# First expert's third block of rows with the rows as the stationary side, a first fill of eight steps, and an order table that reaches into the second expert

## The chip, the cores and the metric

One core of a Trainium2 chip runs the whole program. Its engines are TensorE (PE, with its weight loads as PEld), VectorE (DVE), ScalarE (ACT), GpSimd (POOL) and SyncE (SP, which here only starts loads). Each works through its own list in order and waits on semaphores for the others. The metric is the device time of one execution in microseconds (us), as the median of several runs.

## What is computed

Three stages, each on the output of the one before: attention over a window of 64 positions, a dense layer pair, and a mixture of eight experts, of which each token takes one.

```python
# attention: 4 batches x 8 heads x 576 positions x 64; mask 0 <= i - j < 64
attn = softmax(where(mask, q @ k.T / 8, -1e9)) @ v
x = attn.transpose(0, 2, 1, 3).reshape(2304, 512)
# dense pair: 512 -> 2048 -> 512
h = x @ w_in
x = (h * sigmoid(1.702 * h)) @ w_out
# experts: 8 x (512 -> 1024 -> 512)
logits = x @ w_gate
e = argmax(logits); gate = max of softmax(logits)
out[token] = gate * (max(x @ w1[e], 0) @ w2[e])
```

## The kernel before

All large products are made in three matmuls: each operand is split into a high part and a low part of the 32-bit type that TensorE takes, and hi x hi, hi x lo and lo x hi are added up in PSUM (`mm3`, and `mm3_rows` for several blocks of rows that share a weight). ScalarE makes the high part by a copy, VectorE the low part by a subtraction.

Tokens go through attention and the dense pair in nine chunks of 256. A chunk's sixteen steps are `up_mm` (12 matmuls of 256 columns), the activation (`tanh`, `act`, `g_hi`, `g_lo`) and, two steps later, `down` (6 matmuls of 512 columns). Each chunk's rows are then routed and scattered by POOL to a buffer in HBM, `xbuf`, ordered by expert. The experts are taken in the order of their size, which VectorE works out (`pick_first` after seven chunks, `pick_order` after the last). Their room is `CAPS` = 384, 352, 352, 288, 288, 256, 256, 256 rows.

For an expert, SyncE loads its rows (`load_rows`, into `xg`) and its weights in eight pieces of 512 KB (`load_expert`, into the staging tile `ws`; pieces 0, 1, 4, 5 are of `w1`, the others of `w2`). TensorE transposes the rows (`rows_t`), ScalarE and VectorE split them into `eh` and `el` and the weights into `whi` and `wlo`. Eight steps m follow, one for each 128 of the 1024 hidden units: `e_up` (12 matmuls, weights stationary, as many columns as there are rows), `e_act` and `e_rest` (`gh`, `gl`), and two steps later `e_down` (3 matmuls of 512 columns for each block of 128 rows). `e_out` scales a block by its gate and POOL writes it to the output with an indirect DMA.

The order of the work on PE, ACT, DVE and POOL up to the hand-over is written out by a planner: `part(slot, function, arguments, after=...)` registers each piece of work, and `plan` lays them out one by one by the costs in `MODEL` (engine, us, PSUM banks taken and given back). Behind the planned list a plain loop takes the steps of the experts in order.

The first 256 rows of the first expert belong to chunks that are done early, so `SPLIT` = 7 of its steps are in the planned list with 256 columns, where they fill the time in which the last chunk is routed. Its third block of 128 rows is complete only after the last chunk's scatter (`last_rows`). The loop then takes step 7 with all 384 columns, and for the third block the seven earlier steps once more, over 256 columns of which the first 128 are dropped, with 3 matmuls of `e_down` each:

```python
        steps = [(0, m, 0, CAPS[0], 0) for m in range(SPLIT, NF)]
        steps += [(0, m, CAPS[0] - 256, CAPS[0], 256 - (CAPS[0] - CH)) for m in range(SPLIT)]
        steps += [(e, m, 0, CAPS[e], 0) for e in range(1, E) for m in range(NF)]
```

The second expert's rows and its first two pieces of weights are requested once the planned list is through, behind the readings of the expert order for the experts that are left (`which`); its weights are split inside the loop, one piece a step (`prep_both`).

Of the kernel before, what the change touches and what calls it, by code (L numbers as in the profile page):

```python
# [28 lines left out]
E = 8  # L29
# [11 lines left out]
SPLIT = 7  # L41
# [9 lines left out]
def tile_model(  # L51
# [106 lines left out]
    def mm3_rows(rows, a, b):  # L158

        for o, s, first, _ in rows:  # L160
            nc.tensor.matmul(out=o, lhsT=a[0][:, s], rhs=b[0], start=first, stop=False)  # L161
            nc.tensor.matmul(out=o, lhsT=a[0][:, s], rhs=b[1], start=False, stop=False)  # L162
        for o, s, _, last in rows:
            nc.tensor.matmul(out=o, lhsT=a[1][:, s], rhs=b[0], start=False, stop=last)  # L164
# [230 lines left out]
    def down(c, m):  # L395
        if m == 0:
            y_t[c] = [ps.tile([P, DM], F32, tag="ps", name="y") for _ in range(2)]
        gh, gl = g_t.pop((c, m))
        hi, lo = wout_t[m // 4]
        mm3_rows(  # L400
            [(y_t[c][b], slice(b * P, b * P + P), m == 0, m == NM - 1) for b in range(2)],
            (gh, gl), (hi[:, m % 4, :], lo[:, m % 4, :]),
        )
# [220 lines left out]
    def load_expert(e, i):  # L624

        j, z = divmod(i, 2)
# [12 lines left out]
    def prep_expert(e, i, h, lo_eng):  # L639
        j, z = divmod(i, 2)  # L640
        hi, lo = ew_t[e, j]
        split(hi[:, 2 * z + h], lo[:, 2 * z + h], st_t[e, i][:, h], lo_eng)
# [63 lines left out]
    def e_up(e, m, c0=0, c1=None, skip=0):  # L706
# [14 lines left out]
        eu_t[e, m] = (h, n, skip, c0, c1)  # L721

    def e_act(e, m):
        h, n, skip, c0, c1 = eu_t[e, m]
        if "o" in xp2:
            pool, w, n_b = xp2["o"], CAPS[0], 3
        else:
            pool, w, n_b = gp, CH, 3
        if tail(e):
            n -= TAIL  # L730
            if m == 0:
                gt_t[e] = xp2["o"].tile([P, NF, TAIL], F32, tag="gt", name="gt", bufs=1)
# [52 lines left out]
    def e_down(e, m):  # L785
        done, rows = [], []
        gh, gl, c0, c1 = g_t.pop(("e", e, m))
        hi, lo = ew_t[e, 2 * (m // 4) + 1]
        for b, n in blocks(e):
            if not c0 <= b * P < c1:  # L790
                continue
# [6 lines left out]
            rows.append((o[0:n], slice(b * P - c0, b * P - c0 + n), i == 0, i == NF - 1))  # L798
        mm3_rows(rows, (gh, gl), (hi[:, m % 4, :], lo[:, m % 4, :]))
# [208 lines left out]

    def clear_rows():
        with tc.issue_after(last_w[0].ins):  # L1010
            init_xbuf(yp.tile([P, ROW], F32, tag="ys", name="zt"))
# [7 lines left out]
        top_half: ("ACT", 0.66, 0, 0), join: ("DVE", 0.69, 0, 0), w_hi: ("ACT", 0.66, 0, 0), w_lo: ("DVE", 0.67, 0, 0),  # L1019
        up_mm: ("PE", 1.45, 1, 0), tanh: ("ACT", 0.35, 0, 0), act: ("DVE", 0.37, 0, 1),  # L1020
        g_hi: ("ACT", 0.4, 0, 0), g_lo: ("DVE", 0.4, 0, 0), down: ("PE", 1.4, 0, 0),
# [4 lines left out]
        logits_pe: ("PE", 1.0, 0, 0), lg_out: ("DVE", 0.2, 0, 1),  # L1026
# [4 lines left out]
        e_up: ("PE", 1.45, 1, 0), e_act: ("ACT", 0.4, 0, 0), e_rest: ("DVE", 0.4, 0, 1),  # L1031
        e_down: ("PE", 1.4, 0, 0),
        load_gate: ("SP", 6.0, 0, 0), clear_rows: ("POOL", 1.0, 0, 0), swap_pools: ("NONE", 0, 0, 0),
    }
# [6 lines left out]
    def plan():  # L1041
# [5 lines left out]
        while left:  # L1047
# [3 lines left out]
            for k in left:  # L1051
                eng, cost, take, give = MODEL[k[0]]
                take += 2 * (k[0] in (down, e_down) and k[1][1] == 0)
                if k[0] is logits_pe:
# [144 lines left out]
    for m in range(SPLIT):  # L1199
# [18 lines left out]
    for b, _ in blocks(0)[2:]:  # L1218
        part(SLOTS + SPLIT + 0.5, rows_t, 0, b, after=[(last_rows, ())])
        part(SLOTS + SPLIT + 0.6, rows_hi, 0, b, after=[(rows_t, (0, b))])  # L1220
        part(SLOTS + SPLIT + 0.7, rows_lo, 0, b, after=[(rows_hi, (0, b))])

    with tc.manual_schedule(engines={mybir.EngineType.PE}):
# [9 lines left out]
        p2_cm = pools[0]  # L1233
        xpool_cm.__exit__(None, None, None)
        yt_cm.__exit__(None, None, None)
        gp_cm.__exit__(None, None, None)
        p2o_cm = tc.tile_pool(name="p2o", bufs=1, side="right", reuse_waits="tile")
        xp2["o"] = p2o_cm.__enter__()
        count_rows(*cnt_t["order"])
        with tc.issue_after(rows_in[-1].ins):  # L1240
            load_rows(1)
            for i in range(2):
                load_expert(1, i)
        steps = [(0, m, 0, CAPS[0], 0) for m in range(SPLIT, NF)]
        steps += [(0, m, CAPS[0] - 256, CAPS[0], 256 - (CAPS[0] - CH)) for m in range(SPLIT)]
        steps += [(e, m, 0, CAPS[e], 0) for e in range(1, E) for m in range(NF)]
        for i in range(E * NF + 2):
            if i == 2:
                staged.__exit__(None, None, None)
            e = i // NF  # L1250
            if e < E:
                e_up(*steps[i])
                e_act(*steps[i][0:2])
                e_rest(*steps[i][0:2])
            if i > 1:
                e_down(*steps[i - 2][0:2])
            f = (i - 2) // NF
            if i > 1 and tail(f) and (i - 2) % NF == NF - 1:
# [14 lines left out]
        p2_cm.__exit__(None, None, None)  # L1273
        p2o_cm.__exit__(None, None, None)
# [56 lines left out]
```

## Time and profile before

| | |
|---|---|
| median of 3 runs | 735.07 us (734.48 to 737.21) |
| profiled execution, its own time | 736.32 us |
| its span, first to last instruction | 734.5 us |
| TensorE busy | 711.6 us, 97% |
| VectorE, ScalarE, POOL busy | 470.7, 358.2, 47.0 us |
| granted TensorE clock, mean | 0.998 |

The profiled execution is one of its own; its time is the span and what lies around it. The page has the busy time of each engine, the chain that ended last, and the costliest groups of instructions; other views list the waits, a stretch in order of time, or the loads. A matmul's own length (0.28 us for 256 columns, 0.40 for 512) is not its price: they overlap, and what one adds is the distance to the next one's start.

### The profile page before, as it was taken

The page shows a single profiled execution, that of the slowest core. Times are in us where ns is not written, and L with a number is a line of the kernel's source. Part 1 is how long each engine was busy: PE and PEld are TensorE (multiplying, and loading weights), DVE is VectorE, ACT ScalarE, POOL GpSimd, SP SyncE. Part 2 cuts the span into 40 slices and gives each one's busy share as a digit, 9 for nine tenths or more (in the row PEclk, how much of TensorE's full clock was granted, in tenths as well). Part 3 has the DMA queues.
Part 4 walks back from the last instruction along what each step waited for, and adds up shares of the span by engine and source line. Part 5 has one row for each costly group of instructions (what it writes and reads, how often), then busy time and mean ns, then how long its engine had stood idle before and what let it go on. Part 6 is the DMA issues. An engine that isn't in the chain of part 4 may idle for free.

```text
span 734.5 us, 14397 instructions
## 1 busy us (share of the span) xinstructions
PE 711.6 (97%) x5356; PEld 630.5 (86%) x5357; DVE 470.7 (64%) x1481; ACT 358.2 (49%) x921; POOL 47.0 (6%) x59
## 2 busy tenths in 40 slices
PE   5899999999999999999999999999999999999995
PEld 3789888898898889889989988998888888889995
DVE  5998747977755855946846747853677444858421
ACT  6998746354444435435443524441465433556311
POOL 1000000011001010010010010101100201201111
PEclk9999999999999999999999999999999999999999
DMA  9993793122203202211220001421898528787100
GB/s 340 380 383 152 247 321 122 38 105 105 73 5 105 76 30 77 76 45 62 77 104 1 1 30 58 142 89 44 271 306 278 177 82 309 252 313 248 40 26 27
DMA packets 45370, 103.14 MB, mean 140 GB/s; under 512 B 3951, under 2 KB 12143, under 8 KB 45040
## 3 DMA queue, kind: packets, MB, share of 16 engines
q1 hardware_dynamic: 42304, 92.72, 37.1%
q0 software_dynamic: 2992, 9.46, 3.4%
q8 instruction: 43, 0.70, 0.4%
q14 instruction: 31, 0.25, 0.1%
HBM read 86.39 MB, written 16.03 MB: 139 GB/s over the span
## 4 chain that ended last, share of the span: by engine, by line
PE 78%; issue 10%; DMA 6%; ACT 3%; DVE 1%; SPq 1%; POOL 1%; POOLq 0%; ACTq 0%; DVEq 0%
PE h L154 9%; PE y L161 9%; PE h L156 9%; PE h L155 9%; PE y L162 9%; PE y L164 9%; DMA ws<-in_w 4%; PE t L258 3%; PE eh_ps L154 3%; PE eh_ps L155 3%; PE eh_ps L156 2%; PE s L201 2%; PE o L161 2%; PE o L162 2%; PE o L164 2%
## 5 line engine op out<-in xcount | busy, mean ns | idle before, releaser
L154 PE MATMUL h<-xh,whi 128*128 128x256 f32 x576 | 164.9, 286 | 0.0
L156 PE MATMUL h<-xh,wlo 128*128 128x256 f32 x576 | 162.9, 283 | 0.0
L155 PE MATMUL h<-xl,whi 128*128 128x256 f32 x576 | 162.8, 283 | 0.1
L375 ACT ACTIVATE th<-h 128x256 f32<-128x256 f32 x144 | 54.7, 381 | 137.3 <-PE h L156 131.4
L161 PE MATMUL y<-whi,gh 128*128 128x512 f32 x288 | 116.5, 405 | 0.9 <-ACT gh L386 0.9
L154 PEld LDWEIGHTS h<-xh,whi 128*128 128x128 f32 x576 | 109.6, 190 | 6.8 <-issue 1.9
L162 PE MATMUL y<-wlo,gh 128*128 128x512 f32 x288 | 113.9, 396 | 0.0
L155 PEld LDWEIGHTS h<-xl,whi 128*128 128x128 f32 x576 | 109.7, 190 | 4.7 <-DVE xl L279 0.3
L156 PEld LDWEIGHTS h<-xh,wlo 128*128 128x128 f32 x576 | 109.7, 190 | 0.0
L379 DVE SCALAR_TENSOR_TENSOR th<-th,h 128x256 f32<-128x256 f32 x144 | 60.3, 419 | 67.9 <-ACT th L375 66.9
L436 DVE CUSTOM_DVE_ANT_0 junk<-ys,wg 128x512 bf16<-128x512 f32 x128 | 88.1, 689 | 2.0
L164 PE MATMUL y<-whi,gl 128*128 128x512 f32 x288 | 89.3, 391 | 0.0
L154 PE MATMUL eh_ps<-eh,whi 128*128 128x256 f32 (+3 forms) x284 | 85.4, 301 | 0.7 <-ACT eh L690 0.7
L155 PE MATMUL eh_ps<-el,whi 128*128 128x256 f32 (+3 forms) x284 | 83.6, 294 | 0.3 <-DVE el L697 0.3
L156 PE MATMUL eh_ps<-eh,wlo 128*128 128x256 f32 (+3 forms) x284 | 83.5, 294 | 0.0
L150 DVE TENSOR_TENSOR wlo<-ws,whi 128x1024 fp32r<-128x1024 f32 x56 | 67.9, 1220 | 23.5 <-ACT whi L149 23.2
L386 ACT ACTIVATE gh<-th 128x256 fp32r<-128x256 f32 x144 | 59.4, 415 | 47.7 <-DVE th L379 43.8
L392 DVE TENSOR_TENSOR gl<-th,gh 128x256 fp32r<-128x256 f32 x144 | 60.6, 422 | 28.8 <-ACT gh L386 21.8
L149 ACT ACTIVATE whi<-ws 128x1024 fp32r<-128x1024 f32 x56 | 58.6, 1057 | 38.5 <-DMA ws<-in_w 28.4
L164 PEld LDWEIGHTS y<-whi,gl 128*128 128x128 f32 x288 | 54.1, 188 | 12.5
L226 ACT ACTIVATE pr<-pr,mx 128x128 f32<-128x128 f32 x144 | 55.9, 392 | 17.2 <-DVE mx L216 17.2
L161 PEld LDWEIGHTS y<-whi,gh 128*128 128x128 f32 x288 | 54.5, 189 | 8.5 <-ACT gh L386 1.1
(133 smaller groups left out, 1117.4 us busy)
## 6 DMA issues: line engine op xcount, KB each, us to landing
ws<-in_w SPq DMA_DIRECT2D x64, 512.0 KB, 4.9
qkv<-in_qkv SPq DMA_DIRECT2D x36, 672.0 KB, 5.4
st<-in_w_out SPq DMA_DIRECT2D x16, 511.8 KB, 9.9
st<-in_w_in SPq DMA_DIRECT2D x16, 511.0 KB, 10.3
xbuf<-zt SPq DMA_DIRECT2D x8, 771.0 KB, 13.7
xg<-xbuf SPq DMA_DIRECT2D x17, 257.0 KB, 6.4
raw<-in_w SPq DMA_DIRECT2D x8, 512.0 KB, 9.6
wg<-in_w_gateT SPq DMA_DIRECT2D x2, 1024.0 KB
```

Of the source, the lines that this page charges most:

```text
L149: nc.scalar.activation(out=hi, in_=raw, func=AF.Copy)
L150: lo_eng.tensor_tensor(out=lo, in0=raw, in1=hi.bitcast(F32), op=ALU.subtract)
L154: nc.tensor.matmul(out=o, lhsT=a[0], rhs=b[0], start=first, stop=False)
L155: nc.tensor.matmul(out=o, lhsT=a[0], rhs=b[1], start=False, stop=False)
L156: nc.tensor.matmul(out=o, lhsT=a[1], rhs=b[0], start=False, stop=last)
L161: nc.tensor.matmul(out=o, lhsT=a[0][:, s], rhs=b[0], start=first, stop=False)
L162: nc.tensor.matmul(out=o, lhsT=a[0][:, s], rhs=b[1], start=False, stop=False)
L164: nc.tensor.matmul(out=o, lhsT=a[1][:, s], rhs=b[0], start=False, stop=last)
L379: nc.vector.scalar_tensor_tensor(out=th, in0=th, scalar=1.0, in1=h_t.pop((c, m)), op0=ALU.add, op1=ALU.mult)
L386: nc.scalar.activation(out=gh, in_=th, func=AF.Copy)
L392: nc.vector.tensor_tensor(out=gl, in0=th, in1=gh.bitcast(F32), op=ALU.subtract)
L436: nc.vector.tensor_tensor_reduce(out=junk, in0=ys[:, 0:DM], in1=wg_t[e // 4][:, e % 4, :], scale=1.0, scalar=0.0, op0=ALU.mult, op1=ALU.ad ...
```

## The change

The first expert's first 256 rows now get all eight steps in the planned list. Its third block is computed the other way round: `row_up` keeps the 128 rows stationary and streams 512 columns of `w1` at a time (two halves z, 12 matmuls each), `row_act` takes the activation of that half (128 rows x 512 hidden units) into a tile of the pool `yp`, `row_tr` transposes it back in four pieces of 128x128, `row_gh` and `row_gl` split it, and `row_down` does the usual 3 matmuls for each m. The planned list also takes in the second expert's rows (`next_rows`, `rows_t` and so on), its weights' loads and their splits (`n_hi`, `n_lo`), and the first two loads of the third expert. `load_rows(2)` follows the list, and the loop starts at the second expert. The activations of blocks 0 and 1 and of a third block now lie in tiles of their own (`gh`, `gl` and `g3`), so `e_act` and `e_rest` work in two pieces for the experts with 352 rows. Some costs in `MODEL` are new, by which the planner also sets other parts of the list.

```diff
+GW = CAPS[1]
-SPLIT = 7
...
     def load_expert(e, i):
+        if e == 1:
+            with tc.issue_after(rows_in[-1].ins):
+                fetch_expert(e, i)
+        else:
+            fetch_expert(e, i)
...
+    def n_hi(e, i):
+        j, z = divmod(i, 2)
+        nc.scalar.activation(out=ew_t[e, j][0][:, 2 * z : 2 * z + 2], in_=st_t[e, i], func=AF.Copy)
...
     def e_act(e, m):
...
+        gh, gl = [gp.tile([P, CH], F32R, tag=t, name=t, bufs=3) for t in ("gh", "gl")]
+        gs = [(gh, gl, h[:, 0:CH])]
+        if n > CH:
+            g3 = xp2["o"].tile([P, 2, GW - CH], F32R, tag="g3", name="g3", bufs=3)
+            gs.append((g3[:, 0, 0 : n - CH], g3[:, 1, 0 : n - CH], h[:, CH:n]))
+        for gh, _, x in gs:
+            nc.scalar.activation(out=gh, in_=x, func=AF.Relu)
+        g_t["e", e, m] = (gs, c0, c0 + n)
...
+    def row_up(z):
+        h = rw_t["h", z] = ps.tile([P, 512], F32, tag="ps", name="hr")
+        hi, lo = ew_t[0, 2 * z]
+        eh, el = [t[:, :, 2 * P : 3 * P] for t in ex_t[0][3:5]]
+        for k in range(KD):
+            mm3(h, (eh[:, k], el[:, k]), (hi[:, k], lo[:, k]), k == 0, k == KD - 1)
+
+    def row_act(z):
+        r = rw_t["r", z] = yp.tile([P, ROW], F32, tag="ys", name="hr")[:, 0:512]
+        nc.scalar.activation(out=r, in_=rw_t["h", z], func=AF.Relu)
+
+    def row_tr(z):
+        t = rw_t["t", z] = ps.tile([P, 4, P], F32, tag="ps", name="ht")
+        for i in range(4):
+            nc.tensor.transpose(t[:, i, :], rw_t["r", z][:, i * P : i * P + P], ident)
...
+    def row_down(g):
...
+        for m in (2 * g, 2 * g + 1):
+            hi, lo = ew_t[0, 2 * (m // 4) + 1]
+            mm3_rows(
+                [(eo_t[0, 2][0], rw_t["g", g], slice(m % 2 * P, m % 2 * P + P), m == 0, m == NF - 1)],
+                (hi[:, m % 4, :], lo[:, m % 4, :]),
+            )
...
-        top_half: ("ACT", 0.66, 0, 0), join: ("DVE", 0.69, 0, 0), w_hi: ("ACT", 0.66, 0, 0), w_lo: ("DVE", 0.67, 0, 0),
-        up_mm: ("PE", 1.45, 1, 0), tanh: ("ACT", 0.35, 0, 0), act: ("DVE", 0.37, 0, 1),
+        top_half: ("ACT", 0.78, 0, 0), join: ("DVE", 0.69, 0, 0), w_hi: ("ACT", 0.66, 0, 0), w_lo: ("DVE", 0.67, 0, 0),
+        up_mm: ("PE", 1.44, 1, 0), tanh: ("ACT", 0.35, 0, 0), act: ("DVE", 0.37, 0, 1),
...
-    for m in range(SPLIT):
+    for m in range(NF):
...
+    for i in range(NF + 2):
+        e, z = divmod(i + NF, NF)
+        part(SLOTS + 3.5 + 0.5 * i, load_expert, e, z, after=begin + [
+            (n_lo, (1, i - 4)) if i > 3 else None,
+        ])
...
-        for i in range(E * NF + 2):
-            if i == 2:
+        load_rows(2)
+        for i in range(NF, E * NF + 2):
+            if i == NF + 2:
                 staged.__exit__(None, None, None)
+                count_rows(*cnt_t["order"])
```

TensorE, at the hand-over. Before, the transposes of the first expert's last block of rows (`et<-ident,xg`) have an `e_down` ahead of them (`o`) and the 384-wide `e_up` (`eh_ps`) right behind them:

```order
L164 MATMUL o<-whi,gl 128x512 x2
L684 MATMUL et<-ident,xg 128x128 x4
L154 MATMUL eh_ps<-eh,whi 128x384
L155 MATMUL eh_ps<-el,whi 128x384
L156 MATMUL eh_ps<-eh,wlo 128x384
```

Afterwards two `e_down` and `row_up` (`hr`) follow those transposes, and this is where `row_up` ends; `ht` is what `row_tr` writes, and `et` are by now transposes of the second expert's rows:

```order
L156 MATMUL hr<-whi,el 128x512
L772 MATMUL ht<-ident,hr 128x128 x4
L695 MATMUL et<-ident,xg 128x128 x4
L772 MATMUL ht<-ident,hr 128x128 x4
L695 MATMUL et<-ident,xg 128x96 x4
L161 MATMUL o<-whi,gh 128x512
L162 MATMUL o<-wlo,gh 128x512
L164 MATMUL o<-whi,gl 128x512
```

The narrow `e_up` and `e_down` steps of the third block are gone from TensorE's list, and 24 `hr` matmuls, 8 `ht` transposes and an unbroken run of 24 `o` matmuls stand in their place; the second expert's row transposes moved ahead of its first `e_up`.

ScalarE, in the same place. Before, behind the activations of the planned steps (`gh<-eh_ps`) and the split of the last rows (`eh<-et`), the copies of expert 1's weights (`whi<-ws`) alternate with the narrow activations:

```order
L737 ACTIVATE gh<-eh_ps 128x256 x3
L690 ACTIVATE eh<-et 128x4x128
L737 ACTIVATE gh<-eh_ps 128x384
L149 ACTIVATE whi<-ws 128x1024
L737 ACTIVATE gh<-eh_ps 128x128 x2
L149 ACTIVATE whi<-ws 128x1024
L812 ACTIVATE os<-o,ti 128x512
```

Afterwards (`hr<-hr` is `row_act`, `gh<-ht` is `row_gh`, `os<-o,ti` is `e_out` of the first block):

```order
L747 ACTIVATE gh<-eh_ps 128x256 x4
L701 ACTIVATE eh<-et 128x4x128
L866 ACTIVATE os<-o,ti 128x512
L648 ACTIVATE whi<-ws 128x1024 x2
L767 ACTIVATE hr<-hr 128x512
L701 ACTIVATE eh<-et 128x4x128
L648 ACTIVATE whi<-ws 128x1024
L767 ACTIVATE hr<-hr 128x512
L780 ACTIVATE gh<-ht 128x256
```

Two weight copies now stand ahead of the first `row_act`, and a third one and a row split between the two.

SyncE, behind the load of the first expert's last rows (`xg<-xbuf`). Before, seven readings of the expert order (`TENSOR_LOAD order`) follow it, of which the last two are here, and then the second expert's three row loads and its first weights:

```order
L619 TENSOR_LOAD order
L619 ISA x2
L668 ISA
L668 DMA xg<-xbuf 128x514
L668 ISA
L668 DMA xg<-xbuf 128x514
L668 ISA
L668 DMA xg<-xbuf 96x514
L636 ISA
L636 DMA ws<-in_w 128x2x512
```

Afterwards one reading is left there, and a piece of weights goes ahead of the rows:

```order
L679 DMA xg<-xbuf 128x514
L619 TENSOR_LOAD order
L619 ISA x2
L643 ISA
L643 DMA ws<-in_w 128x2x512
L679 ISA
L679 DMA xg<-xbuf 128x514
```

The other readings moved behind the fourth piece of the second expert's weights, some of them behind the sixth and the seventh.

## Rows read from the trace of the kernel before

**Rows 1.** The page, part 1: busy us, share of the span, instructions.

```profile
PE 711.6 (97%) x5356; PEld 630.5 (86%) x5357; DVE 470.7 (64%) x1481; ACT 358.2 (49%) x921; POOL 47.0 (6%) x59
```

**Rows 2.** Busy time by stretch: length, engines with counts, clock, DMA share, GB/s.

```profile
core 0: us, PE busy (x) PEld busy (x) DVE busy (x) ACT busy (x) POOL busy (x), PEclk, DMA share, GB/s
22.00:43.00 21.00, 18.54 (x213) 15.04 (x205) 19.68 (x70) 19.91 (x63) 0.00 (x0) 1.00 1.06 376
43.00:60.00 17.00, 17.00 (x117) 15.71 (x116) 16.16 (x35) 15.98 (x34) 0.00 (x0) 1.00 1.05 395
60.00:449.00 389.00, 388.91 (x3198) 347.37 (x3197) 262.77 (x967) 186.26 (x567) 14.31 (x14) 1.00 0.25 85
...
545.00:727.10 182.10, 182.10 (x1105) 159.96 (x1103) 95.37 (x166) 79.74 (x128) 20.20 (x17) 1.00 0.54 185
```

**Rows 3.** Waits of TensorE, whole run: total us, times, longest.

```profile
PE s L201 <- DMA qkv<-in_qkv: 7.4, 5, 5.0
...
PE y L161 <- ACT gh L386: 0.9, 1, 0.9
```

**Rows 4.** TensorE in order of time, 507.5 to 545.5 us: start, length, instruction, [idle before].

```profile
507.98 0.39 PE L161 MATMUL o<-whi,gh 128*128 128x512 f32 x1
...
509.36 0.39 PE L161 MATMUL o<-whi,gh 128*128 128x512 f32 x1
...
512.70 0.63 PE L684 MATMUL et<-ident,xg 128*128 128x128 f32 x4 [0.46 <-DMA xg<-xbuf]
514.02 0.44 PE L154 MATMUL eh_ps<-eh,whi 128*128 128x384 f32 x1 [0.69 <-ACT eh L690]
514.74 0.44 PE L155 MATMUL eh_ps<-el,whi 128*128 128x384 f32 x1 [0.29 <-DVE el L697]
...
521.66 0.60 PE L684 MATMUL et<-ident,xg 128*128 128x128 f32 x4
522.01 0.37 PE L154 MATMUL eh_ps<-eh,whi 128*128 128x256 f32 x1
...
524.56 0.50 PE L164 MATMUL o<-whi,gl 128*128 128x512 f32 x1 [0.42 <-DVE gl L744]
...
529.91 0.28 PE L154 MATMUL eh_ps<-eh,whi 128*128 128x256 f32 x1
...
531.31 0.39 PE L161 MATMUL o<-whi,gh 128*128 128x512 f32 x1
...
535.09 0.50 PE L161 MATMUL o<-whi,gh 128*128 128x512 f32 x1 [1.52 <-ACT gh L737]
...
535.90 0.32 PE L154 MATMUL eh_ps<-eh,whi 128*128 128x352 f32 x1
...
537.84 0.40 PE L161 MATMUL o<-whi,gh 128*128 128x512 f32 x1
...
543.07 0.39 PE L161 MATMUL o<-whi,gh 128*128 128x512 f32 x1
```

**Rows 5.** The transposes of rows, whole run: ns min/median/max, first and last start.

```profile
L684 PE MATMUL et<-ident,xg x84: 221/272/300, 480.3 to 690.4; 128*128 128x128 f32 x68, 96*128 96x96 f32 x8, 32*128 32x32 f32 x8
```

**Rows 6.** SyncE in order of time, 509 to 516.5 us, loads alone.

```profile
509.77 0.34 SPq L668 DMA_DIRECT2D xg<-xbuf  x1
...
514.37 1.43 SPq L668 DMA_DIRECT2D xg<-xbuf  x3
...
516.04 0.39 SPq L636 DMA_DIRECT2D ws<-in_w  x1
```

**Rows 7.** The loads into `ws`, whole run, from issue.

```profile
DMA to landing us min/median/max: 3.5/4.9/8.4
```

**Rows 8.** ScalarE in order of time, 508 to 536 us.

```profile
521.99 1.06 ACT L149 ACTIVATE whi<-ws 128x1024 fp32r<-128x1024 f32 x1 [4.51 <-DMA ws<-in_w]
...
523.28 1.06 ACT L149 ACTIVATE whi<-ws 128x1024 fp32r<-128x1024 f32 x1
...
525.76 0.59 ACT L690 ACTIVATE eh<-et 128x512 fp32r<-128x512 f32 x1
```

**Rows 9.** The indirect writes to `out` (256 KB, POOL), whole run, from issue.

```profile
DMA to landing us min/median/max: 3.2/5.7/7.0
```

More of the change, by code (lines that the diff above doesn't have):

```diff
@@ L704, in tile_model, with e_up @@
     eu_t = {}
-    def e_up(e, m, c0=0, c1=None, skip=0):
+    def e_up(e, m, c0=0, c1=None):
         c1 = c1 or CAPS[e]
@@ L1007, in swap_pools, with swap_sides, next_rows @@
         xp2["g"] = pools[0].__enter__()
+    def swap_sides():
+        for cm in (xpool_cm, yt_cm):
+            cm.__exit__(None, None, None)
+        pools.append(tc.tile_pool(name="p2o", bufs=1, side="right", reuse_waits="tile"))
+        xp2["o"] = pools[1].__enter__()
+    def next_rows():
+        with tc.issue_after(rows_in[-1].ins):
+            load_rows(1)
     def clear_rows():
@@ L1030, in tile_model @@
         rows_t: ("PE", 0.5, 1, 0), rows_hi: ("ACT", 0.55, 0, 0), rows_lo: ("DVE", 0.9, 0, 1),
-        e_up: ("PE", 1.45, 1, 0), e_act: ("ACT", 0.4, 0, 0), e_rest: ("DVE", 0.4, 0, 1),
-        e_down: ("PE", 1.4, 0, 0),
+        e_up: ("PE", 1.44, 1, 0), e_act: ("ACT", 0.4, 0, 0), e_rest: ("DVE", 0.4, 0, 1),
+        e_down: ("PE", 1.37, 0, 0),
         load_gate: ("SP", 6.0, 0, 0), clear_rows: ("POOL", 1.0, 0, 0), swap_pools: ("NONE", 0, 0, 0),
+        row_up: ("PE", 2.75, 1, 0), row_act: ("ACT", 0.65, 0, 1), row_tr: ("PE", 0.5, 1, 0),
+        row_gh: ("ACT", 0.42, 0, 0), row_gl: ("DVE", 0.43, 0, 0), row_down: ("PE", 1.37, 0, 0),
+        swap_sides: ("NONE", 0, 0, 0), next_rows: ("SP", 1.0, 0, 0),
+        n_hi: ("ACT", 1.08, 0, 0), n_lo: ("DVE", 1.24, 0, 0),
     }
@@ L1053, in plan @@
                 take += 2 * (k[0] in (down, e_down) and k[1][1] == 0)
+                if k[0] is e_down and k[1][1] == NF - 1:
+                    give = 2
+                if k[0] is row_down:
+                    take, give = int(k[1][0] == 0), int(k[1][0] == 3)
+                if k[0] is row_gl:
+                    give = k[1][0] % 2
                 if k[0] is logits_pe:
@@ L1217, in tile_model @@
     part(SLOTS + 3.1, pick_order, after=[(count, (1,))])
[L1218 to L1221, printed above, removed]
+    R = SLOTS + 6
+    part(R, rows_t, 0, 2, after=[(last_rows, ())])
+    part(R + 0.01, rows_hi, 0, 2, after=[(rows_t, (0, 2))])
+    part(R + 0.02, rows_lo, 0, 2, after=[(rows_hi, (0, 2))])
@@ new lines, in tile_model @@
+    for z in range(2):
+        part(R + 0.1 + z, row_up, z, after=[
+            (rows_lo, (0, 2)), (row_up, (0,)) if z else None,
+            *[(e_lo, (0, 4 * z + i, h)) for i in range(2) for h in range(2)],
+        ])
+        part(R + 0.2 + z, row_act, z, after=[(row_up, (z,))])
+        part(R + 0.3 + z, row_tr, z, after=[(row_act, (z,))])
+    for g in range(4):
+        part(R + 0.4 + g / 2, row_gh, g, after=[
+            (row_tr, (g // 2,)), (e_rest, (0, NF - 1)), (row_gh, (g - 1,)) if g else None,
+            (e_down, (0, 5 + g)) if g < 3 else (row_down, (0,)),
+        ])
+        part(R + 0.5 + g / 2, row_gl, g, after=[(row_gh, (g,))])
+        part(R + 2.5 + g / 2, row_down, g, after=[
+            (row_gl, (g,)), (row_down, (g - 1,)) if g else (e_down, (0, NF - 1)),
+            *[(e_lo, (0, 4 * (g // 2) + 2 + i, h)) for i in range(2) for h in range(2)],
+        ])
@@ L1232, in tile_model @@
             fn(*a)
[L1233 to L1246, printed above, removed]
-        for i in range(E * NF + 2):
-            if i == 2:
+        load_rows(2)
+        for i in range(NF, E * NF + 2):
+            if i == NF + 2:
                 staged.__exit__(None, None, None)
-            e = i // NF
+                count_rows(*cnt_t["order"])
+            e, m = divmod(i, NF)
             if e < E:
[L1252 to L1256, printed above, removed]
+                e_up(e, m)
+                e_act(e, m)
+                e_rest(e, m)
+            if i > NF + 1:
+                e_down(*divmod(i - 2, NF))
             f = (i - 2) // NF
-            if i > 1 and tail(f) and (i - 2) % NF == NF - 1:
+            if i > NF + 1 and tail(f) and (i - 2) % NF == NF - 1:
                 down_tail(f)
```

89 lines of the change are left out of this document (56 added, 33 removed).

## The prediction

> **What bounds the kernel now.** The page's first part comes first: TensorE is busy for 711.6 of the 734.5 us of the span [rows 1], so only two things can save time here: less work on TensorE, or fewer waits of TensorE. The table by stretch says where the rest is [rows 2]. From 43 us to 449 us TensorE has no gap worth naming (17.00 of 17.00, then 388.91 of 389.00), and from 545 us to the end of the work none at all (182.10 of 182.10). What is left is the opening, 22 to 43 us with 18.54 of 21.00, and the hand-over from the first expert to the second, 505 to 545 us, which the next view shows matmul by matmul. The waits of TensorE over the whole run [rows 3] put the opening down to loads of q, k, v above all (7.4 us, of which 5.0 is the first load), and name one wait of 0.9 us on a conversion of `gh`; the lists before and after the change have the same rows around that one, so it stays.
>
> The order in time of the hand-over [rows 4] is the stage that the change rewrites. Brackets there are idle time. The last block's rows arrive at 512.70 us (0.46 idle). Then each step waits for what the step before it just caused: `eh` 0.69, `el` 0.29, `gl` 0.42, `gh` 1.52. From 512.70 to 543.07, where the second expert's first `e_down` starts, 30.37 us pass.
>
> **The change, part by part.** The hand-over is a sum in which both ends are fixed. Up to 512.70 nothing moves: today three `e_down` stand between 507.98 and the transpose of the last rows, afterwards `e_down`, `e_up`, `e_down`. A step of six 512-wide matmuls is 1.38 us (507.98 to 509.36) and a 256-wide `e_up` 1.40 (529.91 to 531.31) [rows 4], so TensorE arrives at 512.14 instead of 512.12 and waits for the same load.
>
> From there to the second expert's first `e_down` the new list holds:
> - transposes of rows, four blocks: 3 x 0.35 (521.66 to 522.01) and the narrower last one at no more than that: 1.40 at most, I take 1.33;
> - two `e_down`: 2.76;
> - `row_up` twice, 24 matmuls of 512 columns. A 512-wide matmul costs 1.38/6 = 0.23 in those `e_down` rows, where its stationary side changes as often as it will here: 5.52;
> - `row_tr` twice, eight transposes of the same 128x128 kind: 0.70;
> - `row_down`, 24 matmuls: 5.52;
> - three `e_up` of the second expert at 1.94 (535.90 to 537.84): 5.82.
>
> That is 21.65 against 30.37: **8.7 us less**. About 4.3 is work: seven 256-wide `e_up` of 1.40 for the third block, and the extra of the one 384-wide step (0.7, in proportion to the 352-wide 1.94), give way to 5.52 + 0.70. The four bracketed waits after 512.70 are 2.9, and the other 1.5 is the slow restart next to each of them. `e_down` 6 and 7 now stand between the transpose and the first use of `eh` and `el`, 2.76 us of cover for the 0.98 that those waits took.
>
> The transposes are where a rule speaks against the change. Four of them take 0.35 us from the first start to the next step's start [rows 4], 88 ns each, although one alone lasts 272 ns [rows 5]: they overlap. The Trainium skill, "TensorE: Matmul & The Clock Gate", Part 4: PE-mode transpose, gives about 275 ns for one in a kernel's context. By that figure eight would cost an estimated 2.2 us in place of 0.70, and the saving would be 7.2. The trace agrees with it as the length of one, not as the price in a row.
>
> **What the new order makes TensorE wait for.** Three steps hang on ScalarE, which works its list in order.
>
> SyncE: today seven readings of the expert list stand between the last rows' load (509.77) and the next load (514.37), 0.6 us each, and the first weights of expert 1 leave at 516.04 [rows 6]. Now one reading stands there. I put the first weight load at 510.8, the three row loads behind it at 0.55 each, the second and third weight loads at 513.0 and 513.6.
>
> ScalarE before `row_act` 0: `e_out`, then `n_hi`(1,0) and `n_hi`(1,1), each waiting for its load. A weight load lands in 4.9 us at the median, 3.5 to 8.4 [rows 7]; today the first one behind three row loads is converted 5.95 after its issue, the next one 1.29 later [rows 6, 8]. So the second lands at about 519.0, is converted by 520.1 (1.06), and `row_act` 0 (0.59, as the 512-wide copy out of PSUM) ends at 520.7 [rows 8]. TensorE wants it after `row_up` 1, at 512.70 + 0.35 + 2.76 + 2.76 + 0.35 + 2.76 = 521.7: hidden by 1 us.
>
> `row_act` 1 stands behind a row conversion (0.59) and `n_hi`(1,2), and it also takes the third buffer of its pool, that of `e_out`'s first block, so it needs that block's write to the output landed. `n_hi`(1,2) ends near 522.3. `e_out` ends at about 516.7, and such a write lands 5.7 after its issue, 3.2 to 7.0 [rows 9]: 522.4. So `row_act` 1 ends near 523.0 and `row_tr` 1, due at 522.4, starts at 523.2: **0.8 us of new wait**. Bounds: 0, if both come at the short ends; 2.6, if the second weight load takes 8.4 (521.4, so `row_act` 0 ends at 523.05 and the rest follows in line). I take 0.8, since the rows of today lie in that same crowd of loads.
>
> `e_act`(1,0) is queued behind `n_hi`(1,7), whose load can leave only when `n_lo`(1,3) has freed the staging tile. That stands behind `row_tr` 1 (done 523.6), some 3 us of ScalarE copies and 1.2 of VectorE: about 528. Landed at 533, converted, `gh` out by 534.8; TensorE wants it at 512.70 + 21.65 + 0.8 = 535.2. Hidden by 0.4; at 8.4 us of landing it would be 3 us late. I take 0.2.
>
> Costed at nothing: the split of `gh` in two for experts 1 and 2 adds 16 copies to ScalarE and 16 subtractions to VectorE, at most 0.59 each [rows 8], 9.4 us spread over 16 steps, in a stretch where ScalarE is busy for 79.74 of 182.10 us [rows 2]; `e_down` comes two steps after its `e_act`. Without that cover each step would be late by a copy. The small VectorE operations of `count_rows`, and its iota on POOL, move behind `row_down` and the first two output writes; only the program's end reads their result, and five of the small ones stand ahead of `n_lo`(1,6), which is not wanted before the fifth `e_down` of expert 1. The tables' new prices (`top_half` 0.78) also reorder the opening.
>
> **The opening.** There the second pair's scores now precede the first `up_mm`, and the conversions shift by a place or two. Up to the point where both lists again hold the same work, ScalarE has the same instructions, and it is busy for 19.91 of 21.00 us between 22 and 43 [rows 2]; the loads are issued in the same order. So at most 1.1 us can be gained, if all its idle time goes. A loss can come where TensorE now meets a load earlier; the qkv waits there are 7.4 - 5.0 = 2.4 in all [rows 3], and I bound a loss by as much again. I take 0 between the two.
>
> **Sum.** 8.7 - 0.8 - 0.2 = 7.7. The profiled execution's span of 734.5 becomes 726.8. Its own time was 736.32 us, 1.8 above the span and 1.25 above the median of the runs, 735.07; with the median as the base the forecast is **727.4**.
>
> **Rivals.**
> - *No new wait.* Loads and the output write come at their short ends: 735.07 - 8.7 = 726.4, with a lucky opening 725.3. For it: `row_act` 0 has 1 us to spare. Against it: weight loads share the stretch with row loads and two output writes. 14%.
> - *Loads or writes late.* The crowd takes 7 to 8 us per load; `row_tr` waits 2 to 2.6 and `e_down`(1,0) up to 3: 729 to 731.5. For it: the bounds of [rows 7, 9]. Against it: the loads start 5 us earlier than today. 16%.
> - *Transposes that do not overlap.* If each of the eight waited for the one before, at 272 ns [rows 5], they would cost 2.2 instead of 0.7, and 6.2 of the 7.7 would stay: 728.9. For it: each pair of four here reads one tile that ScalarE has only just written. Against it: the row transposes of today overlap. 3%. The page of the Trainium skill named above would have it so.
> - *The opening comes undone* (the other side). If ScalarE's list, now with attention ahead of the weight conversions, lets TensorE run dry after 43 us, the saving goes back. It decides against the change only if TensorE becomes saturated more than 7.7 us later than it does today, by 43 us. The room is 1.1 us of idle ScalarE, which speaks for it; the loads, in an unchanged order, speak against it. Loss of 4 to 11: 731.4 to 738.7, or more. 10%, of which 4 slower.
>
> **How the numbers follow.** The forecast has the other 57%, its own range 726.5 to 728.6. The range of 725.4 to 731.2 takes in the first three rivals but for the end of the late loads, and leaves out the opening. Half a per cent, 3.7 us, is what measurement can tell from no change: faster 57 + 14 + 16 + 3 = 90%, within it 6%, slower 4%.
>
> **What would show it.** Right: row transposes of the last block still near 512.7 with a wait of about half a microsecond, no wait before `row_up`, a gap under 2.6 us in front of the second `row_tr`, released by ScalarE; 24 `row_up` matmuls at 0.23 apart; the second expert's first `e_up` near 529.5 instead of 535.90, its first `e_down` near 535.3 instead of 543.07; nothing new after that. Wrong: waits of TensorE on `hr` or on expert 1's `gh` of more than 3 us together, `row_up` slower than 0.23 per matmul, or TensorE idle after 43 us.

## The result, and the profile after

The changed kernel took 728.99 us (median of 4 runs, 728.36 to 730.73) beside 735.45 us for the kernel before, a ratio of 0.9907 with a 95% interval of 0.9885 to 0.9929. Two later comparisons of the same kernel gave 0.9887 (0.9865 to 0.9909) and 0.9907 (0.9891 to 0.9922). Its own median stayed between 728.85 and 728.99 in all three; that of the kernel before was 735.45, 737.22 and 735.80.

The profiled execution took 728.77 us, with a span of 727.1 instead of 734.5. First the page's busy times, which answer to [rows 1]:

```profile
PE 706.0 (97%) x5304; PEld 624.7 (86%) x5305; DVE 471.6 (65%) x1494; ACT 359.1 (49%) x936; POOL 46.7 (6%) x59
```

TensorE is busy for 5.6 us less. Of this, 0.8 lies ahead of 449 us (436.95 of busy time against 437.74), where the end of the work hardly moves, so there it is only idle for longer. Behind 449 us it is busy for 4.8 less, and the other 2.6 of the 7.4 are waits. The stretches, in the columns of [rows 2]:

```profile
22.00:43.00 21.00, 17.71 (x210) 14.47 (x202) 19.37 (x69) 19.42 (x61) 0.00 (x0) 1.00 1.06 377
43.00:60.00 17.00, 17.00 (x120) 15.70 (x115) 16.49 (x34) 15.87 (x35) 0.00 (x0) 1.00 1.05 396
505.00:538.00 33.00, 32.71 (x183) 28.29 (x182) 22.15 (x50) 17.90 (x31) 5.66 (x6) 1.00 0.77 256
```

TensorE is busy for less of the opening, but at 43 us TensorE is saturated again, as before. The hand-over is nearly closed: 0.29 us idle of 33. The list of TensorE's waits shows what is left of them, to be held against [rows 3]:

```profile
PE s L201 <- DMA qkv<-in_qkv: 7.3, 5, 4.9
PE t L244 <- DVE pr L235: 3.6, 5, 1.2
PE y L161 <- ACT gh L386: 0.9, 1, 0.9
...
PE et L695 <- DMA xg<-xbuf: 0.4, 1, 0.4
...
PE ht L772 <- ACT hr L767: 0.3, 1, 0.3
```

The entry `t` behind `pr` is attention in the opening; it was 1.2 us before. And the hand-over in order of time on TensorE, which takes the place of [rows 4]:

```profile
480.76 1.33 PE L695 MATMUL et<-ident,xg 128*128 128x128 f32 x8 [0.40 <-DMA xg<-xbuf]
...
512.97 0.60 PE L695 MATMUL et<-ident,xg 128*128 128x128 f32 x4
513.33 0.48 PE L161 MATMUL o<-whi,gh 128*128 128x512 f32 x1
...
516.18 0.39 PE L154 MATMUL hr<-whi,eh 128*128 128x512 f32 x1
...
518.97 0.60 PE L695 MATMUL et<-ident,xg 128*128 128x128 f32 x4
519.33 0.48 PE L154 MATMUL hr<-whi,eh 128*128 128x512 f32 x1
...
522.21 0.60 PE L772 MATMUL ht<-ident,hr 128*128 128x128 f32 x4
522.64 0.60 PE L695 MATMUL et<-ident,xg 128*128 128x128 f32 x4
523.53 0.66 PE L772 MATMUL ht<-ident,hr 128*128 128x128 f32 x4 [0.29 <-ACT hr L767]
524.02 0.49 PE L695 MATMUL et<-ident,xg 96*128 96x96 f32 x4
524.30 0.48 PE L161 MATMUL o<-whi,gh 128*128 128x512 f32 x1
...
529.87 0.32 PE L154 MATMUL eh_ps<-eh,whi 128*128 128x352 f32 x1
...
535.67 0.39 PE L161 MATMUL o<-whi,gh 128*128 128x512 f32 x1
```

From the last block's transposes to the second expert's first `e_down` (535.67) are 22.70 us; before, they were 30.37. The only wait in it is at the second `row_tr`. The transposes start 0.27 later than before, since a wait of 0.40 for the first rows' load has appeared at 480.76. Behind it the last chunk's scatter starts 0.81 later (505.13 instead of 504.32) and the load of the last rows leaves 0.37 later (510.14 instead of 509.77 [rows 6]). So 30.37 - 22.70 - 0.27 = 7.40, and that is the whole difference of the spans.

### The profile page after: what moved, and what is told of

Same layout as the page of the kernel before. It is cut to its first block, busy times and chain, and to the rows that moved or that the text cites. A ratio compares the mean times of both kernels' runs of the same rounds, so it can differ in the third digit from the quotient of the medians.

```text
span 727.1 us, 14361 instructions
## 1 busy us (share of the span) xinstructions
PE 706.0 (97%) x5304; PEld 624.7 (86%) x5305; DVE 471.6 (65%) x1494; ACT 359.1 (49%) x936; POOL 46.7 (6%) x59
## 4 chain that ended last, share of the span: by engine, by line
PE 83%; issue 8%; DMA 3%; ACT 2%; DVE 2%; POOL 1%; POOLq 0%; ACTq 0%; SPq 0%; DVEq 0%
PE h L154 9%; PE y L161 9%; PE h L156 9%; PE y L162 9%; PE h L155 9%; PE y L164 9%; PE o L161 3%; PE eh_ps L154 3%; PE o L162 3%; PE o L164 3%; PE eh_ps L156 3%; PE eh_ps L155 3%; PE s L201 2%; PE t L258 2%; PE t L244 2%
## 5 line engine op out<-in xcount | busy, mean ns | idle before, releaser
L154 PE MATMUL eh_ps<-eh,whi 128*128 128x256 f32 (+2 forms) x256 | 77.0, 301 | 0.0
L155 PE MATMUL eh_ps<-el,whi 128*128 128x256 f32 (+2 forms) x256 | 75.4, 295 | 0.0
L156 PE MATMUL eh_ps<-eh,wlo 128*128 128x256 f32 (+2 forms) x256 | 75.4, 295 | 0.0
L150 DVE TENSOR_TENSOR wlo<-ws,whi 128x1024 fp32r<-128x1024 f32 x48 | 58.0, 1219 | 19.2 <-ACT whi L149 19.0
L149 ACT ACTIVATE whi<-ws 128x1024 fp32r<-128x1024 f32 x48 | 50.1, 1056 | 26.6 <-DMA ws<-in_w 15.5
```

The source lines that it names most:

```text
L150: lo_eng.tensor_tensor(out=lo, in0=raw, in1=hi.bitcast(F32), op=ALU.subtract)
L154: nc.tensor.matmul(out=o, lhsT=a[0], rhs=b[0], start=first, stop=False)
L155: nc.tensor.matmul(out=o, lhsT=a[0], rhs=b[1], start=False, stop=False)
L156: nc.tensor.matmul(out=o, lhsT=a[1], rhs=b[0], start=False, stop=last)
```

## The experiments

"Theory" is the prediction's account: the work saved by the turned block, the waits closed by the new order, nothing from the opening. Each experiment is the changed kernel with one edit, unless it says otherwise.

**The opening alone.** The table of costs as it was:

```diff
-        top_half: ("ACT", 0.78, 0, 0), join: ("DVE", 0.69, 0, 0), w_hi: ("ACT", 0.66, 0, 0), w_lo: ("DVE", 0.67, 0, 0),
-        up_mm: ("PE", 1.44, 1, 0), tanh: ("ACT", 0.35, 0, 0), act: ("DVE", 0.37, 0, 1),
...
+        top_half: ("ACT", 0.66, 0, 0), join: ("DVE", 0.69, 0, 0), w_hi: ("ACT", 0.66, 0, 0), w_lo: ("DVE", 0.67, 0, 0),
+        up_mm: ("PE", 1.45, 1, 0), tanh: ("ACT", 0.35, 0, 0), act: ("DVE", 0.37, 0, 1),
...
```

> The changed kernel with the six changed prices of the table of costs put back (top_half 0.66, up_mm and e_up 1.45, down and e_down 1.40, logits_pe 1.0), so that the opening is again in the order of before. My theory: the new prices are worth nothing, the whole gain comes from the hand-over between the experts; the span stays within 0.5 us of 727.1 and the wait on gh at about 449 us is reached at the same 449.1 to 449.2. Rival: part of the gain is the opening's; then TensorE gets there 1 us or more later and the span is 728 to 734.

Span 727.4, median 729.07, ratio 0.9887 (0.9858 to 0.9917). The wait at 449 us ends where it does in the changed kernel (450.32) and in the one before (450.39):

```profile
450.29 0.50 PE L161 MATMUL y<-whi,gh 128*128 128x512 f32 x1 [0.91 <-ACT gh L386]
```

So the new opening is worth nothing, as predicted. These costs also put two weight conversions and a `row_gh` between the two `row_act`; the wait at the second `row_tr` is 0.89 there, while the one at 480 is absent, and the two about cancel.

**The turned block alone.** `row_up`, `row_act`, `row_tr` and `row_down` give way to the old way of computing the block, in the same place, with the second expert's splits laid out around it:

```diff
+    def nb_up(m):
...
+                (eh[:, k, P : 3 * P], el[:, k, P : 3 * P]), k == 0, k == KD - 1,
...
```

> The changed kernel, but the third block is computed with the weights stationary, as before: eight steps of twelve 256-wide matmuls of which 128 columns are used, and eight of three 512-wide ones, in the place of row_up, row_tr and row_down. Loads, readings and the eight fill steps stay as in the changed kernel. My theory: the turned block saves work of TensorE; 8 x 1.40 + 8 x 0.69 + three transposes of rows at 1.05 make 17.8 us from the first matmul of the third block (516.2) to the second expert's first e_up, which then starts at 534.0 instead of 529.9: 4.1 us longer, span 731.2. Rival: the gain is in the waits alone and the turned block earns nothing, because its transposes and its wait eat what the narrow steps cost; then the difference is under 1 us.

The order of time, from the first matmul of the block to the second expert's first `e_up`:

```profile
517.36 0.28 PE L154 MATMUL nb<-eh,whi 128*128 128x256 f32 x1
...
535.39 0.32 PE L154 MATMUL eh_ps<-eh,whi 128*128 128x352 f32 x1
```

18.03 us instead of 13.69 (516.18 to 529.87), with no wait in it: 4.3 longer, where 4.1 was expected. Median 732.90, ratio 0.9932 (0.9906 to 0.9958); the kernel with the old costs took 729.07 in the same comparison. That is 3.8 of a gain of 7.7 by the medians, and 4.3 by the trace: about half of the gain is this work.

**The place of the loads.** All readings of the order ahead of the second expert's first weights:

```diff
             with tc.issue_after(rows_in[-1].ins):
+                for x in range(1, E):
+                    which(x)
                 fetch_expert(e, i)
```

> The changed kernel with all seven readings of the expert order ahead of the second expert's first weights, as they stood before: six more readings at 0.6 us delay every load of the second expert by about 3.6 us. My theory: ScalarE works in order, so both weight conversions ahead of row_act 0 come later; the second one starts at about 523 instead of 519.45, the first row_tr at about 524.6 instead of 522.21 and the second at about 526.7 instead of 523.53, so the span grows by 2.5 to 3.6 us (729.6 to 730.7). Rival: the loads are hidden by the work of the third block anyway, and the place of the readings is worth nothing: within 0.5 us.

Median 734.79, ratio 0.997 (0.9949 to 0.999): most of the gain is gone. The mechanism is right and its size is not: 5.8 us more from the last block's transposes to the `e_up` (512.60 to 535.26, against 16.90), not 2.5 to 3.6. TensorE in order of time shows where:

```profile
525.37 0.66 PE L774 MATMUL ht<-ident,hr 128*128 128x128 f32 x4 [2.79 <-ACT hr L769]
...
527.34 0.76 PE L774 MATMUL ht<-ident,hr 128*128 128x128 f32 x4 [0.88 <-ACT hr L769]
...
528.45 0.78 PE L161 MATMUL o<-whi,gh 128*128 128x512 f32 x1
529.02 0.63 PE L162 MATMUL o<-wlo,gh 128*128 128x512 f32 x1
...
535.26 0.32 PE L154 MATMUL eh_ps<-eh,whi 128*128 128x352 f32 x1
```

Up to the second `row_tr` the stretch is 4.2 longer. The two waits are 3.67 us, where the changed kernel waits 0.29; the rest is a new wait of 0.29 for rows at 519.13 and the restarts, the slower matmuls right behind a wait. But then matmuls that take 0.23 elsewhere stand 0.42 to 0.57 apart, and from the second `row_tr` to the `e_up` it is 7.92 instead of 6.34. The windows of that kernel give the granted clock in the column before the DMA share:

```profile
522.00:524.00 2.00, 0.58 (x3) 0.14 (x1) 0.00 (x0) 0.23 (x1) 0.00 (x0) 1.00 1.05 414
524.00:526.00 2.00, 0.63 (x6) 0.63 (x7) 1.14 (x1) 2.00 (x4) 0.00 (x0) 1.00 1.04 402
526.00:528.00 2.00, 1.12 (x10) 0.88 (x9) 1.97 (x6) 2.00 (x4) 0.26 (x1) 0.94 0.69 193
528.00:530.00 2.00, 2.00 (x9) 1.71 (x8) 2.00 (x10) 1.62 (x5) 0.00 (x0) 0.50 0.69 244
530.00:532.00 2.00, 2.00 (x8) 1.58 (x7) 1.83 (x4) 1.53 (x3) 0.00 (x0) 0.71 0.69 245
```

From 522 to 528 us TensorE was busy for 2.33 of 6 us; at the end of this stretch the clock fell to 0.50, which is 1.2 GHz; it rose again between 530 and 532 us, with TensorE at work throughout.

**Is it the clock?** The same kernel with twelve more matmuls in the gap, whose results are overwritten:

```diff
         t = rw_t["t", z] = ps.tile([P, 4, P], F32, tag="ps", name="ht")
+        if z == 0:
...
+            for k in range(KD):
+                mm3(t.rearrange("p i r -> p (i r)"), (eh[:, k], el[:, k]), (hi[:, k], lo[:, k]), k == 0, k == KD - 1)
```

> The kernel with the late loads, and twelve more 512-wide matmuls (2.8 us, of no use to the result) on TensorE in front of the first row_tr, where it waited 2.79 us. The loads and ScalarE's list stay as they were, so row_tr starts when it did, at about 525.4 to 525.6. My theory: the clock granted to TensorE fell to half after that wait (0.50 from 528 to 530 us), which cost 1.6 us after the second row_tr; with TensorE kept busy it stays at 1.00 and the second expert's first e_up comes 1.4 to 1.7 us earlier than in that kernel (535.26), although TensorE does more work. Rival: the slow stretch comes from what waits on ScalarE and VectorE (the splits behind row_tr), and not from the clock; then the e_up does not come earlier, or comes later.

Its order of time on TensorE, and one window of it:

```profile
526.15 0.66 PE L779 MATMUL ht<-ident,hr 128*128 128x128 f32 x4 [0.66 <-ACT hr L769]
...
532.50 0.32 PE L154 MATMUL eh_ps<-eh,whi 128*128 128x352 f32 x1
```

```profile
528.00:530.00 2.00, 2.00 (x10) 1.63 (x9) 1.91 (x6) 1.97 (x5) 0.00 (x0) 1.00 0.57 193
```

The clock stays at 1.00, and the stretch behind the second `row_tr` takes 6.35 again, 1.57 less. With 2.8 us of useless work the kernel is faster: 732.36 us, ratio 0.9941 (0.9924 to 0.9958), against 0.997 (0.9949 to 0.999) without it in an earlier comparison. The two intervals overlap a little, so the 1.57 of the trace is the firmer figure. Its second `row_tr` stood 1.2 earlier too, of which 0.6 is an earlier start of the hand-over and the rest loads that landed sooner; only the 1.57 is the clock's.

**What holds the second `row_act`.**

```diff
-        r = rw_t["r", z] = yp.tile([P, ROW], F32, tag="ys", name="hr")[:, 0:512]
+        if z:
+            r = rw_t["r", z] = xp2["o"].tile([P, 512], F32, tag="hr", name="hr", bufs=1)
+        else:
+            r = rw_t["r", z] = yp.tile([P, ROW], F32, tag="ys", name="hr")[:, 0:512]
```

> The changed kernel with a buffer of its own for the second row_act, which then needs no write to the output to have landed; nothing else moves. My theory: that write is what holds it (0.46 us idle of ScalarE before it); it starts at about 522.4 instead of 522.88, the second row_tr has no wait left (0.29 now, 0.45 with the restart), and the second expert's first e_up comes 0.4 to 0.5 us earlier, at 529.4. Rival: the second row_act is held by the weight conversion in front of it or by the matmuls of row_up; then nothing changes, and the 0.46 us of idle time stay.

ScalarE in the changed kernel and the landing of its first two writes to `out`, then ScalarE with the buffer:

```profile
521.36 1.06 ACT L648 ACTIVATE whi<-ws 128x1024 fp32r<-128x1024 f32 x1
522.88 0.60 ACT L767 ACTIVATE hr<-hr 128x512 f32<-128x512 f32 x1 [0.46 <-PE ht L772]
...
DMA to landing us min/median/max: 5.7/6.0/6.4
```

```profile
522.51 1.06 ACT L648 ACTIVATE whi<-ws 128x1024 fp32r<-128x1024 f32 x1
523.45 0.60 ACT L770 ACTIVATE hr<-hr 128x512 f32<-128x512 f32 x1
```

The idle 0.46 is gone, and the block takes 13.21 us (517.21 to 530.42) instead of 13.69. The view had named TensorE as the releaser. The first write left at 517.11 and landed at about 522.8, if its time is the shorter of the two, 5.7; with the longer, 6.4, `row_act` could not have started at 522.88. In the changed kernel's third profile the same row names the write itself:

```profile
522.59 0.60 ACT L767 ACTIVATE hr<-hr 128x512 f32<-128x512 f32 x1 [0.44 <-DMA out<-os,ti]
```

ScalarE's idle time is nearly the same in all three profiles of the changed kernel (0.46, 0.48, 0.44). What TensorE waits for it at the second `row_tr` is not: 0.45, 0.72 and 0.28, with the restart.

**The price of a transpose.** Each `row_tr` transpose four times:

```diff
-        for i in range(4):
+        for i in 4 * list(range(4)):
```

> The changed kernel with each of the eight transposes of row_tr made four times, 24 more into the same places. My theory: transposes in a row overlap and cost their distance, 0.088 us: 2.1 us more from the first row_tr to the second expert's first e_up (7.7 us in the changed kernel), less what hides the wait of 0.45. Rival: each waits for the one before, at the 272 ns of one alone: 6.5 us more.

```profile
522.60 1.91 PE L772 MATMUL ht<-ident,hr 128*128 128x128 f32 x16
524.34 0.60 PE L695 MATMUL et<-ident,xg 128*128 128x128 f32 x4
524.78 1.91 PE L772 MATMUL ht<-ident,hr 128*128 128x128 f32 x16
...
532.36 0.32 PE L154 MATMUL eh_ps<-eh,whi 128*128 128x352 f32 x1
```

Sixteen take 1.74 us, 0.109 each. From the first `row_tr` to the `e_up` (532.36) it is 9.76 us, against 7.19 in the kernel with its own buffer, which has no wait there either: 2.6 for 24. That is a fifth more than 0.088, and far from 6.5. The rival is out.

**The cover of the split.** `e_down` 6 and 7 ahead of the last block's transposes:

```diff
...
+        late = [(fn, (0, 2)) for fn in (rows_t, rows_hi, rows_lo)]
+        pl = [x for x in pl if x not in late]
+        n = pl.index((e_down, (0, 7))) + 1
+        pl[n:n] = late + [(e_out, (0, b)) for b in range(2)]
```

> The changed kernel with e_down 6 and 7 of the first expert ahead of the last block's row transposes instead of behind them (and the scaling of its first two blocks behind the split of these rows). The work is the same. My theory: those two steps were the cover of the split into eh and el; without it row_up waits for eh and el as the kernel before did, 0.69 and 0.29 of wait and 0.85 + 0.55 with the restarts, and as TensorE comes later to row_tr, the 0.45 there goes: the second expert's first e_up comes 0.9 to 1.4 us later. Rival: the cover is worth nothing, since row_tr waits for ScalarE anyway: the e_up stays within 0.3 us of 529.9.

```profile
518.21 0.50 PE L154 MATMUL hr<-whi,eh 128*128 128x512 f32 x1 [0.69 <-ACT eh L701]
...
518.93 0.50 PE L156 MATMUL hr<-whi,el 128*128 128x512 f32 x1
...
531.84 0.32 PE L154 MATMUL eh_ps<-eh,whi 128*128 128x352 f32 x1
```

The wait for `eh` is back, the one for `el` is not: `row_up` uses `el` in its third matmul, where `e_up` used it in its second. From the end of the wait at 449 us to the `e_up` it is 80.24 us (451.60 to 531.84) instead of 79.55: 0.7 more, less than the 0.9 to 1.4 expected, which had counted a wait for `el` with its restart at 0.55. That the wait at `row_tr` would go, as it did, had been reckoned with.

**Three waits fewer.** On top of the buffer, `e_hi`(0,0,0) goes behind `g_hi` and `tanh`, and a `down` ahead of the transposes at 480; the last two lines are in the first version only:

```diff
...
+            ((e_hi, (0, 0, 0)), (g_hi, (8, 1))),
+            ((tanh, (8, 2)), (g_hi, (8, 1))),
+            ((down, (8, 11)), (up_mm, (8, 14))),
+            ((n_lo, (1, 2)), (row_act, (1,))),
+            ((n_hi, (1, 2)), (row_act, (1,))),
...
```

> The changed kernel with three waits of TensorE taken away by order alone: the first weight conversion of expert 0 (e_hi) goes behind g_hi and tanh of the last chunk (0.91 us of wait at 449, 1.07 with the restart); one down of the last chunk goes ahead of the row transposes that waited for their load at 480 (0.56 + 0.19); and the second row_act has its own buffer and goes ahead of the third weight conversion (0.45 at the second row_tr). My theory: each wait is TensorE's own time, so they add up to 2.2 us: span 724.9, second expert's first e_up at 527.7, and about 0.3% less than the changed kernel. Rival: what follows is tied to the last chunk's scatter, the loads behind it and ScalarE's list, which do not come earlier by as much; then at least half goes back into waits at the last block's transposes or at row_tr, and the span is 726 or more.

More than half of the 2.2 us came back behind the second `row_tr`: from there to the `e_up` (521.26 to 528.90) it is 7.64 instead of 6.34, with two new waits in the list of TensorE's waits:

```profile
PE o L164 <- DVE gl L789: 0.6, 1, 0.6
...
PE o L161 <- ACT gh L783: 0.2, 1, 0.2
```

The weight conversion that no longer stood ahead of `row_act` 1 now stood ahead of `row_gh` 0, and its subtraction ahead of `row_gl` 0. Span 726.4, median 728.66; the changed kernel beside it:

> The changed kernel once more, unaltered, beside the same runs of the kernel before: it gives the gain a second measurement. From the spans (734.5 to 727.1) the ratio should be 0.990; 0.9907 was measured. Rival: the kernel before was read too low by its few runs, and the ratio is nearer 0.988, as the run with the old costs gave.

728.90, both at a ratio of 0.9887, so this version gains nothing that the runs can tell. The ratio of the changed kernel is here on the side of the rival. Then the version with that conversion back in its place, and the changed kernel once more:

> The kernel with fewer waits, but with the third weight conversion back ahead of the second row_act, as in the changed kernel; its own buffer and the two changes of order in the last chunk stay. My theory: the waits of 0.39 and 0.76 at row_down came from that conversion and its subtraction (522.16 on VectorE, ahead of row_gl 0); without them the last block's transposes start at 511.1 and the second expert's first e_up follows 16.5 us later, as with the buffer alone: 527.6, span 725.1, 2.2 us under the changed kernel. Rival: the loads come no earlier than before and row_tr waits for the conversions instead; then the e_up stays at 528.5 or later.

> The changed kernel unaltered, in the same call as the one with two places changed, so that the two are timed beside the same runs of the kernel before: 727.5 to 729.5 us, ratio 0.988 to 0.991, and the wait at the second row_tr between 0.3 and 0.7 us again. Rival to the reading that this wait is the write to the output: it would vary with the loads and be absent in some run.

```profile
510.99 0.66 PE L695 MATMUL et<-ident,xg 128*128 128x128 f32 x4
...
521.69 0.65 PE L775 MATMUL ht<-ident,hr 128*128 128x128 f32 x4 [0.35 <-ACT hr L770]
...
528.00 0.32 PE L154 MATMUL eh_ps<-eh,whi 128*128 128x352 f32 x1
```

The hand-over starts 2.0 earlier than in the changed kernel. The `e_up` comes 17.0 behind its start, where 16.5 was expected: the second weight load landed later in its turn (its conversion starts 7.18 behind the start of the hand-over, 6.48 in the changed kernel), so that 0.35 of wait at `row_tr` came back. Span 725.2 and median 726.95 (ratio 0.9885, 0.9869 to 0.9902) against 727.2 and 728.85: 1.9 us less than the changed kernel, though the two intervals overlap. It is the best version here. In the changed kernel's third profile the wait at the second `row_tr` is 0.28 with its restart, just under the 0.3 to 0.7 expected.

## Why the prediction was right, and where its sizes were off

The sum over the hand-over, term by term, from the order of time above:

| term | predicted | measured |
|---|---|---|
| transposes, of rows and `row_tr` | 1.33 + 0.70 | 2.36 |
| two `e_down` | 2.76 | 2.85 |
| `row_up`, 24 matmuls | 5.52 | 5.67 |
| `row_down`, 24 matmuls | 5.52 | 5.57 |
| three `e_up` of expert 1 | 5.82 | 5.80 |
| wait at the second `row_tr` | 0.8 | 0.45 |
| wait at `e_down`(1,0) | 0.2 | 0 |
| sum | 22.65 | 22.70 |

The second `row_tr` starts 0.89 after the transposes before it; 0.44 is what such a group takes without a wait, so 0.45 is the wait with its restart.

That the sum comes out within 0.05 is in part luck: the terms of work were 0.60 too low together, the two waits 0.55 too high. Of the signs named in advance, one missed: the last block's transposes had no wait ahead of them, because TensorE came to them later than before. The others held, with the `e_up` at 529.87 for 529.5 and the `e_down` at 535.67 for 535.3.

- **Work against waits.** Predicted: 4.3 of work, 2.9 of waits, 1.5 of restarts. With the block turned back, 4.3 is lost, but that it is the same figure is in part chance: the block put back has an eighth narrow `e_up` (1.40) where the kernel before had 0.7 in a wide one, and it has no wait of 0.45 at `row_tr`. An estimate of the work saved is then 4.3 - 0.7 + 0.45, some 4.1. The waits and restarts, of which only the one for `eh` was put back, have the rest: 7.67 - 4.1 + 0.45, some 4.0 for the 4.4 predicted.
- **The transposes.** They overlap, but were priced too low: a group of four takes 0.36 to 0.49 here (the narrower last one 0.28), and the step's error is 0.33 us. The figure that the prediction weighed, about 275 ns in the Trainium skill, "TensorE: Matmul & The Clock Gate", Part 4: PE-mode transpose, agrees with the length of one here (272 ns); four times as many showed that it isn't the price in a row. The Trainium skill gives the figure for bf16 and doesn't say which of the two it is.
- **`row_act` 1.** The chain was right: a weight conversion ended at 522.42 (522.3 predicted), the output write landed at about 522.8 (522.4), `row_act` 1 ended at 523.48 (523.0). The wait was smaller, since TensorE came to its second `row_tr` 0.7 later than the sum said.
- **The opening.** 0 predicted; the wait at 449 us ends 0.07 earlier than before, and with the old costs 0.03 earlier still. The rival's loss of 4 to 11 would make 731.4 to 738.4, not 738.7.
- **Loads late.** This rival did not come up. Its price of 2 to 2.6 us at `row_tr` was too low for loads that come late by their old place in SyncE's list: those cost 5.8, of which 3.67 are waits there and 1.57 is the clock.
- **The base.** 727.4 was 1.6 below the median. Of this, 0.3 is the sum (7.7 against 7.4). The rest is the step "with the median as the base": the sum was made against the profiled execution of 736.32 us and then taken from 735.07, the median of three runs. From 736.32 it would have been 728.6. With 735.45 in the first comparison and 736.73, 737.22 and 735.80 in the later comparisons, the 735.07 was the low one.

What was not foreseen is the 0.27 at the start of the hand-over. The wait of 0.40 at 480 us came in some profiles and not in others. TensorE reached that point at about 480.1 in the third profile of the changed kernel (a wait of 0.57), with the old costs and in the filled kernel (no wait), and in the kernel before at 480.27 (no wait). The order around it is that of before, so it is likely a load's landing; no run here holds that landing fixed.

## What to carry to other kernels

When TensorE is saturated on both sides of a hand-over, add up what the new list holds between two fixed points, at the distance between starts: here each term held within 0.35 us, and the sum, in part by luck, within 0.05. Then look at the engine that works in order behind loads: moving one conversion out of the way of one consumer puts it in the way of the next, as the first attempt at fewer waits showed. And don't price a wait of TensorE by its length alone: one of 2.8 us, with one of 0.9 behind it, cost 1.6 more here through the clock.

## What the runs showed of the hardware

**A wait can cost half as much again.** A wait of 2.79 us, with one of 0.88 soon after it, was followed by matmuls at the lower of the two clocks, and 1.57 us more were lost. Behind the 1.52 in the kernel before, the next `e_up` took 1.94 [rows 4], no more than each of the three in the changed kernel (5.80 in all). The Trainium skill, "TensorE: Matmul & The Clock Gate", Part 1: The HAM clock gate, says that "the default state is throttled, and activity releases the throttle"; the trace agrees on activity, with 0.50 granted at 528 to 530 us in one kernel and 1.00 in the one that filled the gap. A throttled start doesn't show: the granted clock of the changed kernel is 1.00 in its first windows too.

**The same in the opening, in some executions.** In the first profile of the changed kernel the first 44 us run at a clock of 1.00. In the kernel with four times the transposes, the same in the opening, TensorE had less to do between 16 and 18 us (0.39 us busy, against 1.00 in the changed kernel), and the granted clock was 0.50 in each window from 18 to 26 us (the first of them is shown):

```profile
16.00:18.00 2.00, 0.39 (x4) 0.15 (x2) 1.14 (x4) 2.00 (x9) 0.00 (x0) 0.85 1.02 400
18.00:20.00 2.00, 1.70 (x16) 1.40 (x18) 1.69 (x4) 1.51 (x4) 0.00 (x0) 0.50 1.04 425
```

The wait at 449 us ended at 451.54 there, 1.2 later than in the changed kernel. A clock of 0.50 in the opening shows too in the kernels with its own buffer (451.83), without the cover (451.60) and with the old block (451.55), so the spans of such profiles are not compared, only the stretches inside. How much of the 1.2 is the clock's isn't shown. In the filled kernel the clock was 0.50 from 18 to 20 us and 0.68 in the next two, and the wait ended at 450.12. In the second profile of the changed kernel it was 1.00 throughout, and the wait ended late all the same:

```profile
451.02 0.50 PE L161 MATMUL y<-whi,gh 128*128 128x512 f32 x1 [0.91 <-ACT gh L386]
```

The clock is likely a part of the spread between runs of one kernel: of the 16 runs of the changed kernel, the five with a mean granted clock of 0.990 or 0.991 took 729.6 us in the mean, the other eleven 728.7. That the one causes the other was not tried.
